# Gated attention and a two-way maxout layer on one core: fewer score groups of the first sequence computed on both sides of the diagonal, and two weight loads at other times

## The chip, the cores and the metric

The kernel runs on one core of a Trainium2 chip. A core has a matrix engine (TensorE, "PE" in the profile, its weight loads "PEld"), a vector engine (DVE), a scalar engine (ACT), a general engine (GpSimd, "POOL"), an engine that here only issues transfers (SyncE, "SP"), and 16 DMA engines that move data between the memory (HBM) and the on-chip buffer (SBUF), or within SBUF. TensorE writes its results to PSUM, which DVE and ACT read. The metric is the device time of one execution in microseconds (us); a run is repeated and the median is taken.

## The reference

There are eight sequences of 3072 tokens. `u` and `v` have 256 columns, `z` has 64; the layer behind has 1024 hidden columns.

```python
scores = (1 / S) * z @ z.T              # 3072 x 3072 for each of 8 sequences
attn   = maximum(scores, 0) ** 2
x      = u * (attn @ v)                 # 24576 tokens x 256
h1, h2 = x @ w1, x @ w2                 # 24576 x 1024 each
out    = maximum(h1, h2) @ w_out        # 24576 x 256
```

The matrix of scores is symmetric, because both factors are `z`. So is its squared positive part. A block of it that lies on one side of the diagonal, transposed, is the block at the mirrored place. The other identity that the kernel uses is `max(h1, h2) = max(h1 - h2, 0) + h2`: the difference needs only `w1 - w2`, and `h2 @ w_out` needs only the folded matrix `W2o = w2 @ w_out`.

## The kernel before, in words

**Tiles.** Tokens of a sequence are cut into 24 blocks of 128 (`NSB`), and these into six groups of four (`G = 4`, `NG = 6`). A step (`class Step`) is one group of 512 query tokens `s` of one sequence `b`; there are 48 steps. In a step, `xacc0` and `xacc1` in PSUM, one for each half of the 256 columns, add up 24 key blocks: each takes two matmuls 128x128 by 128x512, one for each half (`add`, `attn`). The operand that streams is a tile of squared positive scores; it comes from one of three places: `a_sb`, scored by this step itself (`add_own`); `aT`, scored by an earlier step of the same sequence and transposed by DMA (`add_early`); or `aD`, the diagonal group (`add_diag`).

**Scores.** `scores_pair(b, s, k0)` makes the scores of two key blocks against the 512 queries: two matmuls with 64 rows into one PSUM tile `s_ps`, a Relu on ACT (L218, into `r_sb`), a square on DVE (L221, into `a_sb`), and, if the key group lies behind the query group and is not scored again later, a transposing DMA on SP's queue into `aT` (L226). Pairs are made in windows of three (`WIN = 3`): the matmuls of three pairs back to back, which fill the three PSUM tiles of the pool `mm_psum`. In the first four steps the diagonal group is made by pairs as well (`NDIAG`).

**Who is scored twice.** `direct(b, i, j)` on L186 says which groups above the diagonal are not transposed, but scored again by the later step. In the first sequence these are all six pairs of groups among the first four (`i < j <= NDIR`, `NDIR = 3`): (0,1), (0,2), (0,3), (1,2), (1,3) and (2,3). In the other sequences there are none.

**The layer behind.** When a step has all 24 blocks, `finish` multiplies `xacc` by `uT`, the transposed `u`, on DVE (L268), which gives `xT`. Three steps later (`LAG = 3`) follow `put_d`, 16 matmuls `d_ps` with `w1 - w2`, with their Relu into `g_sb` (L292), and `put_o`, the product with `w_out` and `W2o` (`o_ps`, L323, and the store). `fold_w2o` makes `W2o` once, from `w_out` and from `w2T_sb`, which is `w2` transposed by DMA. The subtraction `w1 - w2` is one DVE instruction (L163).

**Order.** TensorE's order is written out: `work` is the list of its pieces with nominal costs, and `reads` says which score rows a piece needs and how long before it (`LAT_OWN`, `LAT_TURNED`, `LAT_DIAG`). From these, each window gets a place between the pieces, as late as its due time allows and at a distance from the others (`GAP`). In steps 1 to 3 of the first sequence the pieces next to a step's border go one column half after the other (`add_half`). `plan` and `plan_load` give transfers a place by nominal time after the start of a step: `plan_load(0, 0, 7, ...)` is 7 nominal us after step 0 of sequence 0 begins. A load is issued from POOL's queue, behind a one-column copy (`gate`, L83) that waits for the newest tile, so that the load does not start early. Transposes and stores are issued from SP's queue in program order, and one that must wait holds up those behind it. The matmuls, the SP transfers, the gates and the loads are all kept in program order (`pin`); the vector and scalar instructions mostly are not, and a scheduler places them.

Of the kernel before, what the change touches and what calls it, by code (L numbers as in the profile page):

```python
# [11 lines left out]
def kernel(  # L12
# [27 lines left out]
    P = 128  # L40
    NSB = S // P
    G = 4
    WIN = 3
    GW = G * P
    NG = NSB // G
    KD = D // P
    KF = Dff // P
    LAG = 3
    NDIR = 3
# [35 lines left out]
    def load(**kw):  # L85
        pin(nc.gpsimd.dma_start(**kw))
# [69 lines left out]
    w1_sb = consts.tile([P, KD, Dff], bf16)  # L156
    w2_sb = consts.tile([P, KD, Dff], bf16)
# [26 lines left out]


    def direct(b, i, j):  # L186
        return b == 0 and i < j <= NDIR


    def score(q, out_ps, j, k, s, q0, n):  # L190
# [13 lines left out]
    def scores_pair(b, s, k0):  # L204
        q = seqs[b]
        s_ps = mm_psum.tile([P, 2, GW], fp32, name="s_ps", tag="mm")
        for j in range(2):
            score(q, s_ps[:, j, :], j, k0 + j, s, 0, G)
        yield
        a_sb = apool.tile([P, 2, GW], bf16, name="a_sb")  # L210
        r_sb = apool.tile([P, 2, GW], bf16, name="r_sb", bufs=3)

        head = b == 0 and s == 0 and k0 < 10
        keep = pin if head else lambda ins: None
        if head and k0 in (2, 6):
            keep(nc.vector.tensor_single_scalar(out=r_sb, in_=s_ps, scalar=0.0, op=ALU.max))  # L216
        else:
            keep(nc.scalar.activation(r_sb, s_ps, AF.Relu))  # L218
        if head and k0 < 4:
            yield  # L220
        keep(nc.vector.tensor_mul(a_sb, r_sb, r_sb))  # L221
        gj = k0 // G
        if gj > s and not direct(b, s, gj):
            if (s, gj) not in q.T:
                q.T[s, gj] = tpool.tile([P, G, G, P], bf16, name="aT")
            turn(  # L226
                q.T[s, gj][:, ds(k0 - G * gj, 2), :, :].rearrange("p k q x -> p (k q) x"),
                a_sb.rearrange("p j q -> p (j q)"),
            )
        yield a_sb  # L230
# [123 lines left out]
    class Step:  # L354
        def __init__(self, b, s):
            self.b, self.s, self.q = b, s, seqs[b]
            self.xacc = None
            self.n = [0] * KD
            self.diag = not (b == 0 and s <= NDIAG)
            self.rows = ([None] if self.diag else []) + [  # L360
                k0
                for k0 in range(0, NSB, 2)
                if k0 // G > s or direct(b, k0 // G, s) or (k0 // G == s and not self.diag)
            ]
            self.early = [i for i in range(s) if not direct(b, i, s)]
            self.scored = {}
# [11 lines left out]
                self.n[dc] += 1  # L378
            attn(self.q, k, moving, self.xacc, dcs, n == 0, n == NSB - 1)

        def add_early(self, k):
            i, qb = divmod(k, G)
            self.add(k, self.q.T[i, self.s][:, :, qb, :])

        def add_own(self, k, dcs=range(KD)):
            self.add(k, self.scored[k - k % 2][:, k % 2, :], dcs)

        def add_half(self, ks, dc):
            for k in ks:
                self.add_own(k, [dc])  # L390

        def add_diag(self, j):
            self.add(G * self.s + j, self.scored[None][:, j, :, :])
# [26 lines left out]
    LAT_OWN, LAT_TURNED, LAT_DIAG = 2900, 9000, 10000  # L420

    def put(ns, shares, fn, reads=()):
        work.append((ns, shares, fn, reads))

    def put_early(st, ks):
        for k in ks:
            i = k // G
            rows = [((NG * st.b + i, k0), LAT_TURNED) for k0 in (G * st.s, G * st.s + 2)]
            put(432, False, lambda st=st, k=k: st.add_early(k), rows)

    def put_d(n):
        if n >= 0:
            for _ in range(KF // 2):
                put(864, True, steps[n].piece_d)

    def put_o(n, split=False):
        if n >= 0:
            for _ in range(G // 2):
                put(2180, True, lambda: steps[n].piece_o(split))

    for n, st in enumerate(steps):
        b, s = st.b, st.s
        if n:
            put(0, False, steps[n - 1].finish)
        put(0, False, st.begin if n else lambda: None, "begin")
        early = [G * i + j for i in st.early for j in range(G)]

        within = {}
        lat = LAT_OWN if n > LAG else 6 * 432
        if s == 0:  # L450
            put_o(n - LAG)
        elif s == NG - 1:
            put_d(n - LAG)
            put_early(st, early[: len(early) // 2])
            put_o(n - LAG)
            put_d(n - LAG + 1)
            put_early(st, early[len(early) // 2 :])
        elif early:
            put_d(n - LAG)
            put_early(st, early[:-2])  # L460
            put_o(n - LAG)
            put_early(st, early[-2:])
        elif n == LAG:
            within = {
                5: lambda: put_d(0),
                9: lambda: (put(1800, True, fold_w2o), put_o(0)),
            }
        own = [k0 for k0 in st.rows if k0 is not None]
        for i, k0 in enumerate(own):
            if i in within:  # L470
                within[i]()
            if not early and n <= LAG and i in ((0, 1) if n else ()) + (len(own) - 2, len(own) - 1):


                if i in (0, len(own) - 2):
                    ks = [own[i], own[i] + 1, own[i + 1], own[i + 1] + 1]
                    for dc in range(KD):
                        put(
                            864,
                            False,  # L480
                            lambda st=st, ks=ks, dc=dc: st.add_half(ks, dc),
                            [((n, own[i]), lat), ((n, own[i + 1]), lat)],
                        )
                continue
            for k in (k0, k0 + 1):
                put(432, False, lambda st=st, k=k: st.add_own(k), [((n, k0), lat)])
        if st.diag:
            for j in range(G):
                put(432, False, lambda st=st, j=j: st.add_diag(j), [((n, None), LAT_DIAG)])
# [50 lines left out]
    for w in reversed(range(len(windows))):  # L540
        limit = min([limit] + [due[r] for r in windows[w] if r in due])
        found = [i for i in spots if begins[i] <= limit]
        i = found[-1] if found else 0
# [11 lines left out]
    def plan(b, s, us, is_load, fn):  # L555
        transfers.append((start_of[b, s] + us * 1000, len(transfers), is_load, fn))

    def plan_load(b, s, us, fn):
        plan(b, s, us, True, fn)
# [14 lines left out]
    def fetch_v(b, i):  # L574
        load_v(b, seqs[b].v, i * G, G)

    for n, st in enumerate(steps):
        b, s = st.b, st.s
# [4 lines left out]
        if s == 0 and b + 1 < B:  # L583
            c = b + 1
# [7 lines left out]
            plan(b, *zT_at, False, lambda c=c: turn_z(c))  # L592
            for i, at in enumerate(v_at):
                plan_load(b, *at, lambda c=c, i=i: fetch_v(c, i))
    plan_load(0, 0, 7, lambda: load(out=w2_sb, in_=moe_w2.rearrange("(c p) f -> p c f", p=P)))
    plan_load(0, 1, 3, lambda: load(out=w1_sb, in_=moe_w1.rearrange("(c p) f -> p c f", p=P)))
    plan_load(0, 2, 9, lambda: load(out=w_out_sb, in_=moe_w_out.rearrange("(c p) d -> p c d", p=P)))
    plan(0, 2, 2, False, turn_w2)
    plan(0, 2, 6, False, subtract_weights)
# [84 lines left out]
```

## Time and profile before

| what | value |
|---|---|
| median of three runs | 981.61 us (981.32 to 990.35) |
| the profiled execution | 981.29 us |
| its span, from first to last instruction | 979.5 us |
| TensorE busy | 968.7 us, 99% |
| DVE busy | 432.2 us, 44% |
| ACT busy | 442.6 us, 45% |
| POOL busy | 77.7 us, 8% |
| granted TensorE clock | 1.00 |
| matmuls of scores of pairs, 128x512 into `s_ps` (with the diagonal's) | 696 |
| transposes into `aT` | 228 |

The span is what the profile can place; 1.8 us of the execution lie around it. An engine's busy time counts each moment once, however many of its instructions overlap. The timeline view merges like instructions that follow one another: start, length, engine, line, operation, output and inputs, count. The view of the transfers gives for each group of DMA issues the size and the time from issue to landing, that is until the data is in place and a waiting engine may go on.

In the first sequence the work of a step takes 13.8 us on TensorE as long as no piece of the layer behind is in it: step 1 begins at about 23.5 us, step 2 at 37.3 us, step 3 at 51.1 us.

### The profile page before, as it was taken

The numbers are of one execution on the slowest core, as the hardware profiler recorded it, in microseconds if no ns is written. First come the engines' busy times: TensorE is split into PE (matmuls) and PEld (weight loads), VectorE is DVE, ScalarE is ACT, GpSimd is POOL, SyncE is SP. The second block draws the span as 40 slices with busy tenths as digits, with TensorE's granted clock in tenths as the row PEclk, the third lists the DMA queues.
The fourth block names the chain that finished last, engine by engine and source line by source line (L and its number), as shares of the span: only waits on it lengthen the run. The fifth ranks groups of instructions, "written<-read, shape, count | busy, mean of one in ns | idle before, by whom it ended". The sixth has DMA issues, their size and how long they took to land.

```text
span 979.5 us, 14514 instructions
## 1 busy us (share of the span) xinstructions
PE 968.7 (99%) x5662; PEld 510.3 (52%) x5743; DVE 432.2 (44%) x681; ACT 442.6 (45%) x500; POOL 77.7 (8%) x228
## 2 busy tenths in 40 slices
PE   9999999999999999999999999999999999999998
PEld 3355545555455554555545564455545555445556
DVE  6654444443544435433445334444345443554322
ACT  6853454334643355433554335533355433654322
POOL 2011000110001100010000100011000110000000
PEclk9999999999999999999999999999999999999999
DMA  9999599987999969897788979889778796796621
GB/s 151 171 161 187 103 182 150 164 149 123 175 160 144 155 123 177 150 170 128 151 156 144 179 119 157 148 153 181 135 147 149 136 187 127 149 161 118 109 66 65
DMA packets 378517, 143.46 MB, mean 146 GB/s; under 512 B 356944, under 2 KB 358608, under 8 KB 378448
## 3 DMA queue, kind: packets, MB, share of 16 engines
q1 hardware_dynamic: 361888, 112.78, 61.5%
q0 software_dynamic: 16560, 29.74, 21.6%
q8 instruction: 45, 0.74, 0.3%
q14 instruction: 24, 0.20, 0.1%
HBM read 59.77 MB, written 25.17 MB: 87 GB/s over the span
## 4 chain that ended last, share of the span: by engine, by line
PE 99%; issue 1%; DVE 0%; ACT 0%
PE xacc L74 52%; PE o_ps L74 21%; PE d_ps L74 17%; PE s_ps L74 8%; PE w2o_ps L74 0%; ACT r_sb L218 0%; DVE r_sb L216 0%; PE tpz L134 0%; DVE a_sb L221 0%; DVE o_sb L317 0%; DVE blank L333 0%
## 5 line engine op out<-in xcount | busy, mean ns | idle before, releaser
L74 PEld LDWEIGHTS <-v_sb 128*128 128x128 bf16 x2304 | 215.9, 98 | 277.7 <-issue 41.1
L218 ACT ACTIVATE r_sb<-s_ps 128x1024 bf16<-128x1024 f32 x258 | 248.6, 1023 | 111.4 <-PE s_ps L74 111.2
L221 DVE TENSOR_TENSOR a_sb<-r_sb 128x1024 bf16<-128x1024 bf16 x260 | 179.4, 691 | 212.9 <-ACT r_sb L218 208.9
L74 PE MATMUL xacc<-a_sb,v_sb 128*128 128x512 bf16 x997 | 231.3, 379 | 2.5 <-issue 0.2
L74 PE MATMUL xacc<-aT,v_sb 128*128 128x512 bf16 x912 | 216.5, 379 | 0.0
L74 PE MATMUL o_ps<-w_out_sb,g_sb 128*128 128x256 bf16 x1536 | 199.1, 273 | 0.0
L74 PE MATMUL d_ps<-xT,w_sb 128*128 128x512 bf16 x751 | 172.7, 379 | 0.9
L74 PEld LDWEIGHTS <-g_sb 128*128 128x128 bf16 x1536 | 149.9, 98 | 27.6
L292 ACT ACTIVATE g_sb<-d_ps 128x1024 bf16<-128x1024 f32 x96 | 98.3, 1024 | 138.8 <-PE d_ps L74 138.8
L292 DVE TENSOR_SCALAR g_sb<-d_ps 128x1024 bf16<-128x1024 f32 x96 | 117.4, 1223 | 84.7 <-PE d_ps L74 81.3
L323 ACT COPY o_sb<-o_ps 128x512 f32<-128x512 f32 x94 | 55.1, 586 | 178.2 <-PE o_ps L74 178.2
L268 DVE SCALAR_TENSOR_TENSOR xT<-xacc,uT 128x512 bf16<-128x512 f32 x96 | 62.0, 683 | 137.4 <-PE xacc L74 137.4
L74 PEld LDWEIGHTS <-w_sb 128*128 128x128 bf16 x768 | 75.1, 98 | 88.7
L74 PE MATMUL s_ps<-zT 64*128 64x512 bf16 (+3 forms) x696 | 89.2, 359 | 0.1
L246 ACT ACTIVATE r_sb<-s_ps 128x896 bf16<-128x896 f32 x44 | 40.3, 917 | 97.9 <-PE s_ps L74 97.9
L74 PE MATMUL xacc<-aD,v_sb 128*128 128x512 bf16 x331 | 79.9, 379 | 2.6 <-issue 2.2
L74 PE MATMUL o_ps<-W2o_sb,xT 128*128 128x256 bf16 x384 | 73.3, 273 | 0.0
L248 DVE TENSOR_SCALAR r_sb<-s_ps 128x384 bf16<-128x384 f32 x44 | 24.6, 558 | 95.3 <-PE s_ps L74 95.3
L74 PEld LDWEIGHTS <-zT 64*128 64x128 bf16 x696 | 27.3, 94 | 62.6 <-issue 50.5
L83 POOL COPY gate_sb<-g_sb 128x1 bf16<-128x1 bf16 x44 | 8.3, 188 | 407.8 <-DVE g_sb L292 238.5
L74 PEld LDWEIGHTS <-xT 128*128 128x128 bf16 x384 | 37.6, 98 | 4.3
L83 POOL COPY gate_sb<-a_sb 128x1 bf16<-128x1 bf16 x48 | 9.7, 202 | 271.8 <-DVE a_sb L221 271.8
(37 smaller groups left out, 143.3 us busy)
## 6 DMA issues: line engine op xcount, KB each, us to landing
out_dram<-o_sb SPq DMA_DIRECT2D x47, 512.0 KB, 4.1
v_sb<-in_v_dram POOLq DMA_DIRECT2D x48, 256.0 KB, 5.9
u_sb<-in_u_dram POOLq DMA_DIRECT2D x48, 256.0 KB, 5.3
aT<-a_sb SPq DMA_TRANSPOSE x228, 3.6
z_sb<-in_z_dram POOLq DMA_DIRECT2D x7, 384.0 KB, 7.5
aD<-aD SPq DMA_TRANSPOSE x132, 2.4
w_sb<-in_moe_w_dram POOLq DMA_DIRECT2D x2, 512.0 KB, 7.5
uT<-u_sb SPq DMA_TRANSPOSE x48, 4.3
```

What stands on the lines that cost most here:

```text
L74: pin(nc.tensor.matmul(*args, **kw))
L83: pin(nc.gpsimd.tensor_copy(gate_sb, tile_ap))
L218: keep(nc.scalar.activation(r_sb, s_ps, AF.Relu))
L221: keep(nc.vector.tensor_mul(a_sb, r_sb, r_sb))
L246: nc.scalar.activation(r_sb, s_ps[:, 0:7, :], AF.Relu)
L248: nc.vector.tensor_single_scalar(out=r2_sb, in_=s2_ps[:, 2:5, :], scalar=0.0, op=ALU.max)
L268: nc.vector.scalar_tensor_tensor(out=xT[:, dc, :].rearrange("p (t q) -> p t q", q=P), in0=xacc[dc].rearrange("p (t q) -> p t q", q=P), sca ...
L292: nc.any.tensor_single_scalar(out=g_sb[:, nb : nb + 2, :], in_=d_ps, scalar=0.0, op=ALU.max)
L323: nc.any.tensor_copy(o_sb[:, ds(2 * th, 2), :], o_ps[:, :, :D])
```

## The change

Three things are edited.

1. `direct` now holds only for neighbours: (0,1), (1,2) and (2,3). The three groups farther from the diagonal, (0,2), (0,3) and (1,3), are scored once, by the earlier step, and transposed by DMA into `aT` for the later one. So steps 2 and 3 of the first sequence have "early" rows, as later steps have.
2. The order of pieces in those steps follows from that. Step 2 begins with the four blocks that it takes from `aT`, one column half after the other. Step 3 begins with `put_d(0)`, then six of its eight early blocks, then `fold_w2o` and `put_o(0)`, then the last two early blocks, and its own rows last. Before, step 3 began with own rows, and had `put_d(0)` after five pairs of own rows and `fold_w2o` and `put_o(0)` after nine.
3. The load of `w2` is planned 2 us after the start of step 1 and not 7 us after the start of step 0; the load of `w1` 9 us after the start of step 1 and not 3 us.

```diff
     def direct(b, i, j):
-        return b == 0 and i < j <= NDIR
+        return b == 0 and j == i + 1 and j <= NDIR
...
-        def add_early(self, k):
+        def add_early(self, k, dcs=range(KD)):
             i, qb = divmod(k, G)
-            self.add(k, self.q.T[i, self.s][:, :, qb, :])
+            self.add(k, self.q.T[i, self.s][:, :, qb, :], dcs)
...
         def add_half(self, ks, dc):
             for k in ks:
-                self.add_own(k, [dc])
+                (self.add_early if k // G in self.early else self.add_own)(k, [dc])
...
+    def reads_of(st, k, lat):
+        n, i = NG * st.b + st.s, k // G
+        if i in st.early:
+            return [((n - st.s + i, k0), LAT_TURNED) for k0 in (G * st.s, G * st.s + 2)]
+        return [((n, k - k % 2), lat)]
...
+    def put_border(st, ks, lat):
+        reads = sum((reads_of(st, k, lat) for k in ks), [])
+        for dc in range(KD):
+            put(864, False, lambda dc=dc: st.add_half(ks, dc), reads)
...
-        elif early:
+        elif n >= LAG:
             put_d(n - LAG)
             put_early(st, early[:-2])
+            if n == LAG:
+                put(1800, True, fold_w2o)
             put_o(n - LAG)
             put_early(st, early[-2:])
-        elif n == LAG:
-            within = {
-                5: lambda: put_d(0),
-                9: lambda: (put(1800, True, fold_w2o), put_o(0)),
-            }
...
+        else:
+            ks = (early + own)[:G] if n else []
+            if ks:
+                put_border(st, ks, lat)
+            early, own = early[G:], own[len(ks) if not early else 0 :]
+            put_early(st, early)
+        tail = own[-G:] if n + 1 < LAG else []
+        for k in own[: len(own) - len(tail)]:
+            put(432, False, lambda st=st, k=k: st.add_own(k), reads_of(st, k, lat))
+        if tail:
+            put_border(st, tail, lat)
...
-    plan_load(0, 0, 7, lambda: load(out=w2_sb, in_=moe_w2.rearrange("(c p) f -> p c f", p=P)))
-    plan_load(0, 1, 3, lambda: load(out=w1_sb, in_=moe_w1.rearrange("(c p) f -> p c f", p=P)))
+    plan_load(0, 1, 2, lambda: load(out=w2_sb, in_=moe_w2.rearrange("(c p) f -> p c f", p=P)))
+    plan_load(0, 1, 9, lambda: load(out=w1_sb, in_=moe_w1.rearrange("(c p) f -> p c f", p=P)))
```

The counts of instructions differ by this: 12 score matmuls of 64 rows and their 12 weight loads fewer on TensorE, six Relu fewer on ACT, six squares fewer on DVE, six transposes into `aT` more on SP. The 24 matmuls of those blocks into `xacc` read `aT` in place of `a_sb`. From step 4 on the order on every engine is the old one, but for a few gates, loads and one store that stand a few places away.

More of the change, by code (lines that the diff above doesn't have):

```diff
@@ L423, in put @@
         work.append((ns, shares, fn, reads))
+    def reads_of(st, k, lat):
[3 more added lines that the diff above has]
+        return [((n, k - k % 2), lat)]
     def put_early(st, ks):
         for k in ks:
-            i = k // G
-            rows = [((NG * st.b + i, k0), LAT_TURNED) for k0 in (G * st.s, G * st.s + 2)]
-            put(432, False, lambda st=st, k=k: st.add_early(k), rows)
+            put(432, False, lambda k=k: st.add_early(k), reads_of(st, k, 0))
+    def put_border(st, ks, lat):
+        reads = sum((reads_of(st, k, lat) for k in ks), [])
+        for dc in range(KD):
+            put(864, False, lambda dc=dc: st.add_half(ks, dc), reads)
     def put_d(n):
@@ L446 @@
         early = [G * i + j for i in st.early for j in range(G)]
-        within = {}
+        own = [k for k0 in st.rows if k0 is not None for k in (k0, k0 + 1)]
         lat = LAT_OWN if n > LAG else 6 * 432
@@ L457 @@
             put_early(st, early[len(early) // 2 :])
-        elif early:
+        elif n >= LAG:
             put_d(n - LAG)
             put_early(st, early[:-2])
+            if n == LAG:
+                put(1800, True, fold_w2o)
             put_o(n - LAG)
             put_early(st, early[-2:])
-        elif n == LAG:
-            within = {
-                5: lambda: put_d(0),
-                9: lambda: (put(1800, True, fold_w2o), put_o(0)),
-            }
[L468 to L486, printed above, removed]
+        else:
[9 more added lines that the diff above has]
+            put_border(st, tail, lat)
         if st.diag:
```

## The prediction

> **What bounds the kernel now.** I read the page first: the busy line, the chain, and the group of the score matmuls.
>
> ```profile
> PE 968.7 (99%) x5662; PEld 510.3 (52%) x5743; DVE 432.2 (44%) x681; ACT 442.6 (45%) x500; POOL 77.7 (8%) x228
> ...
> PE 99%; issue 1%; DVE 0%; ACT 0%
> ...
> L74 PE MATMUL s_ps<-zT 64*128 64x512 bf16 (+3 forms) x696 | 89.2, 359 | 0.1
> ```
>
> The chain that ended last is TensorE from start to end. So time falls by whatever TensorE work goes, unless TensorE then waits for something. The 696 score matmuls, 359 ns each, occupy 89.2 us: 0.128 us each, because the two of a pair, on 64 rows each, lie beside one another.
>
> Then the sums by stage, for steps 1 and 2 of the first sequence, as the change is all in the first 75 us:
>
> ```profile
> 23.50:37.30 13.80, 13.75 (x75) 5.22 (x72) 9.41 (x15) 11.42 (x13) 1.63 (x4) 1.00 1.04 163
> 37.30:51.10 13.80, 13.75 (x75) 5.21 (x72) 10.46 (x16) 11.42 (x13) 0.75 (x2) 1.00 1.24 183
> ```
>
> After the length stand the busy times of PE, PEld, DVE, ACT and POOL, the granted clock (1.00), the DMA share and GB/s. PE is full. ACT is at 11.42 of 13.80, but PE does not wait for it. DMA is the other resource without room: the packets' times sum to 1.04 and 1.24 of sixteen engines, which means that they overlap and hinder each other.
>
> **What goes.** The timeline of TensorE shows one period of a step:
>
> ```profile
> 33.33 0.82 PE L74 MATMUL s_ps<-zT 64*128 64x512 bf16 x6
> 34.09 2.76 PE L74 MATMUL xacc<-a_sb,v_sb 128*128 128x512 bf16 x12
> 36.78 0.82 PE L74 MATMUL s_ps<-zT 64*128 64x512 bf16 x6
> ```
>
> A window of three pairs holds PE from 33.33 to 34.09, 0.76 us; the 12 accumulating matmuls take 2.69. The change takes out six pairs, which are two windows: 2 x 0.76 = **-1.52 us**. (By the page's 0.128 us it is 12 x 0.128 = 1.54.) The matmuls into `xacc` stay, and read `aT` at the same price: 12 of them lie between 96.03 and 98.71 us, 2.68. Six Relu of 1023 ns and six squares of 691 ns go from engines that PE does not wait for: nothing.
>
> **What is added: six transposes on SP, and reads of them.** The nearest rows are in SP's own timeline and the transfers:
>
> ```profile
> 26.86 1.31 SPq L77 DMA_TRANSPOSE uT<-u_sb  x1
> 30.47 9.98 SPq L77 DMA_TRANSPOSE aT<-a_sb  x4
> 40.55 1.41 SPq L77 DMA_TRANSPOSE uT<-u_sb  x1
> 42.05 4.42 SPq L77 DMA_TRANSPOSE w2T_sb<-w_sb  x1
> ```
>
> Undisturbed, SP issues one in 1.29 us (median of the view of `aT` up to 75 us) and it lands 3.3 us later (its minimum). Beside loads, four take 9.98 us, 2.5 each, and land up to 8.7 us after issue. So six more cost SP 7.7 to 15 us before 50 us. Nothing on PE shows unless a reader comes first. The readers, by the changed order and the rows of before:
>
> - *Group (0,2)*. Read at the start of step 2, 37.5 us. Its rows are squared by 14 us, but SP first issues `uT` of step 0 at 15.03, as that waits for its load. Then the two go out by 16.4 + 2 x 2.5 = 21.4 and land by 30. Free.
> - *Groups (0,3), (1,3)*. Read from 53 us in step 3. At 2.5 us each all eight of step 0 are out by 36.4 and the two of (1,3) by 42.7, landed by 51.4. Free.
> - *Buffers of `a_sb`* (18). A square must wait for the transposes of the tile that lay there 18 tiles earlier: the 23rd square, at 32.3, for the first transpose, landed by 28; the 30th, at 40.2, for the last of step 0, landed at 36.4 + 4.4 = 40.8 at the slow rate and 32 at the fast. At most 0.6 us, on DVE; I take nothing.
> - *`uT` of step 2*. Queued behind everything above, and step 3's `xacc` waits for the product with it. Step 2 ends at 49.8 and `put_d(0)` covers 3.5 us, so the landing is needed by 51.9. At the fast rate it is issued at 35 (the last square of step 1 ends at 33.96), at the slow one, 16 issues after 15.03, at 54, and lands at 58; between, near 42, with landing at 47. From 0 to 6 us; I take 0, as `w2`'s load no longer lies beside step 0's transposes (two of those took 2.3 and 4.1 us to issue while it ran, the undisturbed 1.29).
> - *`w2T`*. It follows `uT`, takes 6.5 us to land, and is needed at 56.7. 0 to 6 us, the same queue; I take 0.
>
> **What moves.** `put_d(0)` stood at 56.52 us. Now it follows directly on the last 24 matmuls of step 2: 44.44 + 24 x 0.224 = 49.8, so 6.7 us earlier, while the loads it needs are later.
>
> - *`w1`*. The gate now stands on the third tile of the window at 33.33, squared at 37.62. POOL is free then, so the load goes out at 38.2 instead of 31.04. The subtraction keeps its place on DVE, behind the same nine squares:
>
> ```profile
> 47.07 0.69 DVE L221 TENSOR_TENSOR a_sb<-r_sb 128x1024 bf16<-128x1024 bf16 x1 [0.29 <-ACT r_sb L218]
> 47.68 1.22 DVE L163 TENSOR_TENSOR w_sb<-w_sb 128x2048 bf16<-128x2048 bf16 x1
> ```
>
> It starts at 47.7 and ends at 48.9; the first `d_ps` comes at 49.8. So `w1` must land by 48.5, 10.3 us after issue. The two loads of this size in the transfers before, at 20.69 and 31.04 us:
>
> ```profile
> w_sb<-in_moe_w_dram POOLq DMA_DIRECT2D x1, 512.0 KB, 6.2
> ...
> w_sb<-in_moe_w_dram POOLq DMA_DIRECT2D x1, 512.0 KB, 8.8
> ```
>
> It lands between 44.4 and 47.0, nearest the second, which also had transposes beside it (one took 8.2 us to land). No stall, with 1.5 us to spare. Behind the waiting subtraction DVE holds the two products of step 2, and PE waits for the subtraction itself. Cover gone, it costs the excess one for one: at 12 us to landing, 1.7.
> - *`w2`* goes out behind the load of `u` at 28 instead of 20.69 and lands by 37: early enough.
> - *`fold_w2o`* moves from 64.29 to 56.7 (49.8 + 3.46 of `d_ps` + 4 matmuls 0.9 + a window 0.76 + 8 matmuls 1.79). `w_out`'s gate takes the tile squared at 47.8, not 51.5, and the load goes out at 48.4. Its own row before is 7.9, which gives 56.3; with 8.8 it is 57.2. From nothing to 0.5 us of stall, more if the queue is worse; I take **+0.4**, as step 2's four transposes will lie beside it.
> - *The window after `put_d(0)`* comes after 4 matmuls and not 8. Its third pair needs the PSUM tile of the last `d_ps`; DVE's Relu of that (0.2 us after the matmuls, 1.23 long) ends at 54.7, when the pair is due. **+0.1**.
> - The store of step 0, the next loads of `z`, `v` and `u`: some us earlier, each with 10 us or more before its reader. Nothing. After step 4 all orders are as before.
>
> Sum against the profiled execution: 981.29 - 1.52 + 0.4 + 0.1 = 980.27. The median, 981.61, stands 0.32 above the profiled one, so I say **980.6**.
>
> **The Trainium skill** has two rules here that the numbers above do not use. "DMA: Bandwidth & Descriptors", section "Anatomy of one DMA", fits a load from POOL as about 2.0 us plus its bytes over 436 GB/s. An estimate by it, for the 1 MB that `w1` is in HBM, is 4.4 us; the trace has 6.2 and 8.8, so the measurement decides, and by the page no load would ever be late and the sum would be 979.9. The same page, section "Issuing engines are not separate DMA queues", speaks against the change: SP's transposes and POOL's loads share the same 16 DMA engines. The trace agrees (8.8 for the load beside three transposes).
>
> **Rivals.**
>
> *B. The transposes jam the DMA engines, and TensorE waits at about 50 us.* Place: `put_d(0)` for `w1`, or the first `xacc` of step 3 for `uT`. For it: the DMA share of 1.24, and 2.5 us per transpose. Against it: `w2` and `w1` are now apart, and no PE wait for a DMA shows today. It decides from 1.5 us of stall; the slow rate throughout gives 58 + 0.7 of the product against 53.3, 5.4 us, so 981.6 - 1.5 + 5.4 = 985.5, slower than before; half of that gives 982.8. "TensorE: Matmul & The Clock Gate", Part 1, says that an idle window of about 3.4 us halves the clock; no run here shows it (clock 1.00 in every row), and it would add about 2 us to the longest stall.
>
> *C. Nothing gained: what PE saves turns into small waits* (`w_out`, PSUM, DVE), since these are each within 1 us of due. 981.3 to 981.9. For it: ACT at 83% of a step, and window after window close to due. Against: today these waits sum to 2.5 us of `xacc` in the whole run.
>
> *D. The gain whole*: no wait at all. 981.61 - 1.52 = 980.1; with each window's switch saved as well (16 `d_ps` matmuls take 3.46 us, 0.216 each; the period of 3.45 less 12 of those is 0.86) 979.9.
>
> **How the numbers follow.** Forecast (a stall of 0.2 to 1.2) 0.40, D 0.22, C 0.13, B 0.22, and 0.03 for a jam over 10 us. The range drops the upper end of B and the 0.03: low 979.3 (D, less 0.5 for the spread of medians), high 984.0. About 1% is what a measurement of this kernel can tell from no change; all cases but the last are within it: faster 0.01 and slower 0.01 for what no case holds, slower 0.03 for the jam, same 0.95.
>
> **What would show it.** Right: PE busy about 1.5 us less, 684 score matmuls and 234 transposes; `d_ps` first at about 49.8 us, `fold_w2o` at 56.7; the subtraction at 47.7 with no DMA named before it. Wrong: an idle PE between 49 and 58 us, with DVE's L163 or L268 named as releaser and a load or `uT` behind that; a `w1` load that takes over 10 us; or transposes that SP issues at over 2 us each up to 50 us.

## The result, and the profile after

The changed kernel is slower: 992.17 us in the median of ten runs (987.61 to 996.7, and one far outlier of 1692, at a granted clock of 0.56 over the whole execution), against 981.7 for the kernel before. The ratio is 1.0095, with a 95% interval from 1.0066 to 1.0124. The forecast was 980.6 with a range from 979.3 to 984.0, so time and sign were wrong. The profiled execution took 995.36 us, its span is 993.6, which is 14.1 us more than before. It is the second longest of the nine without the outlier, so its waits are probably longer than those of a typical execution.

The page of the changed kernel: the busy line, the chain, and the groups of the accumulation that reads `aT` and of the product with `uT`.

```profile
PE 973.0 (98%) x5650; PEld 511.3 (51%) x5731; DVE 427.6 (43%) x675; ACT 436.8 (44%) x494; POOL 78.3 (8%) x228
...
PE 93%; DMA 3%; issue 1%; SPq 1%; DVE 1%; ACT 1%; POOL 0%; DVEq 0%; POOLq 0%; ACTq 0%
...
L74 PE MATMUL xacc<-aT,v_sb 128*128 128x512 bf16 x936 | 223.5, 380 | 5.7 <-DVE xT L268 5.7
...
L268 DVE SCALAR_TENSOR_TENSOR xT<-xacc,uT 128x512 bf16<-128x512 f32 x96 | 61.8, 683 | 147.6 <-PE xacc L74 127.7
```

Two things show at once. The chain was 99% TensorE, and is 93% with 3% of DMA in it. And TensorE is busy 4.3 us *longer*, with 12 matmuls fewer, worth 1.5 us: so its work was stretched by 5.8 us. The rest of the 14.1 us, 9.8, is idle time. These three numbers are the whole account: -1.5 + 5.8 + 9.8 = 14.1.

Where the idle time lies is told by the waits of the first 130 us (who waited for whom: sum, times, longest):

```profile
DVE xT L268 <- DMA uT<-u_sb: 11.9, 3, 6.7
...
PE xacc L74 <- DVE xT L268: 5.7, 4, 3.1
PE xacc L74 <- DMA aD<-aD: 3.7, 1, 3.7
```

and by TensorE's timeline at these places:

```profile
37.48 0.82 PE L74 MATMUL s_ps<-zT 64*128 64x512 bf16 x6
40.46 1.02 PE L74 MATMUL xacc<-aT,v_sb 128*128 128x512 bf16 x4 [2.16 <-DVE xT L268]
41.66 1.02 PE L74 MATMUL xacc<-aT,v_sb 128*128 128x512 bf16 x4 [0.17 <-DVE xT L268]
...
52.87 3.62 PE L74 MATMUL d_ps<-xT,w_sb 128*128 128x512 bf16 x15
59.58 0.38 PE L74 MATMUL xacc<-aT,v_sb 128*128 128x512 bf16 x1 [3.09 <-DVE xT L268]
60.18 1.26 PE L74 MATMUL xacc<-aT,v_sb 128*128 128x512 bf16 x3 [0.22 <-DVE xT L268]
...
102.36 2.72 PE L74 MATMUL xacc<-aD,v_sb 128*128 128x512 bf16 x6 [3.72 <-DMA aD<-aD]
104.88 5.25 PE L74 MATMUL d_ps<-xT,w_sb 128*128 128x512 bf16 x16
```

Steps 2 and 3 cannot start to accumulate, because DVE waits for the transposed `u` of the step before; step 4 cannot end, because its diagonal tiles have not come back from the transpose. The sums by stage after the second and third of these stalls show the other loss, in the third number from the end, the granted clock:

```profile
59.60:65.40 5.80, 5.41 (x18) 1.46 (x17) 4.66 (x6) 2.85 (x3) 0.00 (x0) 0.71 1.29 156
...
102.40:110.00 7.60, 7.60 (x23) 2.79 (x23) 2.51 (x3) 1.72 (x2) 0.00 (x0) 0.62 0.75 178
```

A clock of 0.71 over 5.8 us and of 0.62 over 7.6 us is 1.7 + 2.9 us of lost clock; before, it was 1.00 in every row. In the last rows 16 `d_ps` matmuls took 5.25 us, not 3.62. Some of the rest lies at the start: the first `xacc` of step 0 came at 8.87 us and not 8.18. That differs from execution to execution: over the thirteen profiles here it lies between 8.07 and 9.30 us.

Why `uT` is late stands in SP's own timeline:

```profile
16.63 13.06 SPq L77 DMA_TRANSPOSE aT<-a_sb  x8
29.78 3.34 SPq L77 DMA_TRANSPOSE uT<-u_sb  x1
33.21 15.20 SPq L77 DMA_TRANSPOSE aT<-a_sb  x6
48.51 4.75 SPq L77 DMA_TRANSPOSE uT<-u_sb  x1
53.35 5.50 SPq L77 DMA_TRANSPOSE w2T_sb<-w_sb  x1
```

Step 0's eight transposes went out in 13.06 us, 1.6 each. Step 1's six took 15.20, 2.5 each, and `uT` of step 2 left at 48.51 and landed 9.8 us later, at 58.3. In the view of the transfers, at 42 to 44 us, issue to landing was this:

```profile
w_sb<-in_moe_w_dram POOLq DMA_DIRECT2D x1, 512.0 KB, 8.0
aT<-a_sb SPq DMA_TRANSPOSE x1, 12.1
...
u_sb<-in_u_dram POOLq DMA_DIRECT2D x1, 256.0 KB, 11.1
aT<-a_sb SPq DMA_TRANSPOSE x1, 12.4
```

The load of `w1` and that of `u` for step 3, 2.5 us behind it, lay beside the last transposes of step 1. Each of those took 12 us where an undisturbed one takes 3.2.

### The profile page after: what moved, and what is told of

It reads as the page before. It is cut to its first block, busy times and chain, and to the rows that moved or that the text cites. A ratio compares the mean times of both kernels' runs of the same rounds, so it can differ in the third digit from the quotient of the medians.

```text
span 993.6 us, 14489 instructions
## 1 busy us (share of the span) xinstructions
PE 973.0 (98%) x5650; PEld 511.3 (51%) x5731; DVE 427.6 (43%) x675; ACT 436.8 (44%) x494; POOL 78.3 (8%) x228
## 4 chain that ended last, share of the span: by engine, by line
PE 93%; DMA 3%; issue 1%; SPq 1%; DVE 1%; ACT 1%; POOL 0%; DVEq 0%; POOLq 0%; ACTq 0%
PE xacc L74 49%; PE o_ps L74 21%; PE d_ps L74 16%; PE s_ps L74 7%; DMA w2T_sb<-w_sb 1%; DMA uT<-u_sb 1%; DMA aD<-aD 1%; SPq L77 1%; ACT r_sb L218 1%; DVE a_sb L221 0%; DMA o_sb<-in_z_dram 0%; PE w2o_ps L74 0%; DVE r_sb L216 0%; PE tpz L134 0%; DVE xT L268 0%
## 5 line engine op out<-in xcount | busy, mean ns | idle before, releaser
L218 ACT ACTIVATE r_sb<-s_ps 128x1024 bf16<-128x1024 f32 x252 | 243.0, 1023 | 118.2 <-PE s_ps L74 116.7
L221 DVE TENSOR_TENSOR a_sb<-r_sb 128x1024 bf16<-128x1024 bf16 x254 | 175.0, 691 | 220.5 <-ACT r_sb L218 216.4
L74 PE MATMUL xacc<-aT,v_sb 128*128 128x512 bf16 x936 | 223.5, 380 | 5.7 <-DVE xT L268 5.7
L74 PE MATMUL xacc<-a_sb,v_sb 128*128 128x512 bf16 x975 | 225.3, 379 | 2.4 <-issue 0.2
```

The source lines that it names most:

```text
L74: pin(nc.tensor.matmul(*args, **kw))
```

## The experiments

**First question: the transposes or the loads?** Two theories. Theory 1: six more transposes are too much for the queue wherever the loads are. Theory 2: the loads of `w1` and `w2`, which the change moved in beside the transposes, make the jam. Four kernels take the parts apart.

*The changed kernel, loads at the old places* (`e1_old_load_times`):

```diff
-    plan_load(0, 1, 2, lambda: load(out=w2_sb, ...
-    plan_load(0, 1, 9, lambda: load(out=w1_sb, ...
+    plan_load(0, 0, 7, lambda: load(out=w2_sb, ...
+    plan_load(0, 1, 3, lambda: load(out=w1_sb, ...
```

> The changed kernel with the loads of w1 and w2 back at their old places. Theory 1 (six more transposes are too much for SP's queue wherever the loads lie): the uT products of steps 1 and 2 still come late, 986 to 994 us. Theory 2 (the load of w2, moved beside the transposes of uT of step 1, and that of w1, moved beside step 2's, make the jam): uT of step 1 lands before 38 us, no PE idle time before step 3, 980 to 983 us.

Measured: 985.93 us, ratio 1.0045 (1.0023 to 1.0067). Better than the changed kernel, but slower than before. The profile has one stall of TensorE for a late `uT`, 3.95 us at step 2, with the clock at 0.63 for the 4.6 us that follow, and 0.9 us for `w_out`. `uT` of step 1 left SP at 33.8, behind eight transposes that the load of `w2` had slowed, and landed at 41.5; it is needed at 38. Neither theory's range holds the median. The late `uT` of step 1 is theory 1's wait; that of step 2, which theory 1 had late as well, came in time.

*The kernel before, with only the loads moved* (`e2_loads_only`): the reverse edit on the old kernel.

> The kernel before with the loads of w1 and w2 at their new places and nothing else changed. Theory 1: with four transposes per step the queue has room; 981 to 982.5 us. Theory 2: uT of step 1 or 2 lands late as in the changed kernel and PE waits at the start of steps 2 or 3; 984 to 992 us.

Measured: 999.14 us, ratio 1.0158 (1.0118 to 1.0198). The half of the change that I had priced at nothing costs more alone than the whole change. No transpose is added here, and yet:

```profile
44.08 7.84 SPq L77 DMA_TRANSPOSE w2T_sb<-w_sb  x1
52.01 8.06 SPq L77 DMA_TRANSPOSE aT<-a_sb  x4
60.16 4.35 SPq L77 DMA_TRANSPOSE uT<-u_sb  x1
64.60 23.55 SPq L77 DMA_TRANSPOSE aT<-a_sb  x4
```

This is SP's timeline. Four transposes take 23.55 us to issue, 5.9 each. The backlog that began behind `w1` meets the loads of `w_out`, `u`, `z` and `v` one after the other, and never drains: from 75 to 85 us the DMA share is 1.38 and only 90 GB/s move, against 234 in the kernel before in these ten microseconds (first this run, then the kernel before; the DMA share and GB/s stand last):

```profile
75.00:85.00 10.00, 9.92 (x53) 4.10 (x51) 6.52 (x12) 4.57 (x5) 1.44 (x4) 1.00 1.38 90
75.00:85.00 10.00, 10.00 (x59) 4.71 (x58) 7.11 (x14) 4.77 (x6) 1.62 (x5) 1.00 1.19 234
```

In this stretch the engines were busier and moved less. TensorE pays at 89 us (3.9 us for `aT`) and at 106 us (6.9 us for `aD`), long after the loads that began it.

*The changed kernel without its six transposes* (`e3_no_far_transposes`): the far groups come from a tile of zeros.

```diff
-        if gj > s and not direct(b, s, gj):
+        if b == 0 and s + 1 < gj <= NDIR:
+            q.T[s, gj] = far_sb
+        elif gj > s and not direct(b, s, gj):
```

> The changed kernel without its six transposes: the three far groups are read from a tile of zeros, so their part of the sum is left out; the matmuls and the load times are those of the changed kernel. Theory 1: no late uT, the 1.5 us of the two windows is gained whole, 980 to 981 us. Theory 2: uT of step 1 still waits behind the load of w2, 984 to 990 us.

Measured: 985.72 us, ratio 1.0037 (1.0018 to 1.0057), single runs from 981.4 to 990.1. Theory 2's range, but by another wait: `uT` of step 2 landed at 53.0 and stalled TensorE by 0.2 us only. The loss came 40 us later: 2.75 us for `aD` at 94.7, and a clock of 0.54 in the 3.5 us behind it. So the new load places alone keep the gain from coming.

*The kernel before plus the six transposes* (`e4_before_plus_six`), into tiles that nobody reads:

```diff
-        if gj > s and not direct(b, s, gj):
+        if gj > s and (gj > s + 1 or not direct(b, s, gj)):
```

> The kernel before with the six transposes added, into tiles that nobody reads; scores, order and load times are the old ones. Theory 1: uT of steps 1 or 2 lands late, 984 to 992 us. Theory 2: the queue carries them, at most 1 us, 981.5 to 982.5 us.

Measured: 986.4 us; ratio 1.0024, with an interval (0.9966 to 1.0082) that does not tell it from no change. Its profile has one stall, at the start of step 2, for `uT` of step 1:

```profile
37.09 0.82 PE L74 MATMUL s_ps<-zT 64*128 64x512 bf16 x6
40.80 1.02 PE L74 MATMUL xacc<-a_sb,v_sb 128*128 128x512 bf16 x4 [2.88 <-DVE xT L268]
```

All five executions, 985.0 to 990.1, lie above the median of the kernel before, 982.2. Both theories were half right. The transposes with the old loads cost a wait of 3 to 4 us at one place. The new load places cost much more than that in the old order of pieces (`e2_loads_only`) and as much in the new one (985.72 in `e3_no_far_transposes`, 985.93 in `e1_old_load_times`), at places that wander.

**Second question: is anything else in the change slow, and is it the loads in flight or the transposes by themselves?**

*The order alone* (`e5_order_alone`): no far transposes, loads at the old places.

> The changed kernel without its six transposes (the three far groups are read from a tile of zeros, so their part of the sum is left out) and with the loads of w1 and w2 at the old places. What is left of the change is the two windows less and the new order of pieces. Theory (both the transposes and the new load places fill the DMA queues, and nothing else costs): no late uT, 979.8 to 981.0 us, 1.2 to 1.9 below before. Rival (the new order itself waits, for w_out, PSUM or DVE): 981.5 us or more.

Measured: 980.79 us against 982.08 for the kernel before on the same chip, 1.3 below; ratio 0.9992 (0.9983 to 1.0001). The interval just holds no change. The profile has no wait of TensorE for a transfer but 0.3 us for `w_out`. Its span is that of the kernel before, 979.5 us, but its first `xacc` came at 9.30 us and not 8.18; from there on it is 1.1 us shorter, near the 1.5 of the sum less that wait. So the new order itself costs nothing that shows.

With this run there are four medians for the changed order: 980.79 with neither the six transposes nor the new load places, 985.93 with the transposes alone, 985.72 with the load places alone, and 992.17 with both. Each costs about 5 us alone, and a little over 6 beside the other.

*Six transposes, but `w1` and `w2` never loaded* (`e8_no_weight_loads`): constants are written on chip in their place.

> The changed kernel with its six transposes, but w1 and w2 are set to constants on chip and never loaded, so the layer behind computes with other weights. Theory (a load in flight beside the transposes makes these slow): SP issues them at 1.3 us each, uT of steps 1 and 2 land in time, 980 to 983 us. Rival (six more transposes are too much by themselves): late uT as before, 986 us or more.

Measured: 981.04 us, and 979.79 in the profiled execution, whose span is 978.0: 1.5 below the 979.5 of before, the whole gain. The ratio is 1.001 (0.9983 to 1.0037), as three of ten executions take 988 to 992. SP's timeline in this run, to be laid beside that of the changed kernel:

```profile
16.69 12.91 SPq L77 DMA_TRANSPOSE aT<-a_sb  x8
29.70 3.19 SPq L77 DMA_TRANSPOSE uT<-u_sb  x1
32.98 8.16 SPq L77 DMA_TRANSPOSE aT<-a_sb  x6
41.24 2.59 SPq L77 DMA_TRANSPOSE uT<-u_sb  x1
```

The same six transposes of step 1 need 8.16 us and not 15.20, and `uT` of step 2 leaves 7.3 us earlier. So the six transposes are not too much by themselves in this execution; it is the loads of `w1` and `w2` in flight beside them that make them slow. What delays the three long executions is not shown, as none of them was profiled.

**Third question: is it one transfer at the wrong place in the queue, or the sum of transfers?** Here `uT` for steps 1 to 3 is issued some five transposes earlier.

```diff
-        plan(b, s, 1, False, lambda b=b, s=s: turn_u(b, s))
+        early_u = b == 0 and 0 < s <= 3
+        plan(b, s - early_u, 3 if early_u else 1, False, lambda b=b, s=s: turn_u(b, s))
```

*With the old load places* (`e6_ut_early_old_loads`):

> The changed kernel with the loads at the old places, and the transposes of u for steps 1 to 3 of the first sequence issued from SP some five transposes earlier. Theory (late uT at the end of SP's queue is what the readers wait for, not a lack of DMA in sum): the stall of 3.9 us at step 2 and the halved clock behind it go, 980.5 to 982 us. Rival (the sum of DMA work is too much): the wait moves to aT, w2T, w_out or aD, 984 us or more.

*With the new ones* (`e7_ut_early`):

> The changed kernel with its own load places and the transposes of u for steps 1 to 3 issued some five transposes earlier. Theory (late uT): the stalls of 2.3 and 3.3 us at steps 2 and 3 go, 983 to 987 us, with a wait left for aD at about 100 us. Rival (sum of DMA work): as the changed kernel, 988 us or more.

Measured: 986.31 us, ratio 1.0044 (1.0025 to 1.0064), and 990.14, ratio 1.0111 (1.0069 to 1.0152). TensorE waited for `uT` no more in either profile, but for `w2T`, 9.1 and 7.6 us. The timeline of the first:

```profile
55.12 1.90 PE L74 MATMUL xacc<-aT,v_sb 128*128 128x512 bf16 x8
66.09 3.59 PE L74 MATMUL w2o_ps<-w_out_sb,w2T_sb 128*128 128x256 bf16 x16 [9.07 <-DMA w2T_sb<-w_sb]
```

`w2T` had kept its place in SP's queue, behind 14 transposes into `aT` as in the changed kernel. In the first run it was issued at 51.9 us, between the loads of `w_out` (49.1) and `u` (54.4), and took 14.2 us to land; in `e1_old_load_times` it went out at 50.3, before `w_out`, and took 4.4. It landed at 66.0 and 64.3 us, near the 65.4 of the changed kernel, where the earlier stalls had hidden it. The rival held: the other order of this queue chose who was late.

*Two loads apart* (`e9_u3_later`): the kernel before with the new places of `w1` and `w2`, but the load of `u` that went out 3.3 us behind `w1` is planned 5 us later.

> The kernel before with the loads of w1 and w2 at the new places (the run that took 991 to 1001 us), and the load of u for step 3, which there went out 3.3 us behind w1's, moved 5 nominal us later. Theory (the transposes starve while loads follow one another without a break; uT of step 2 was caught behind w1 and u): uT of step 2 lands by 50 us, no pile-up behind it, 982 to 986 us. Rival (the place of w1's load alone does it): 990 us or more.

Measured: 984.76 us; ratio 1.0009 (0.9971 to 1.0047), where it had been 1.0158. Its executions scatter from 981.3 to 997.1. `uT` of step 2 landed at 50.7 in place of 52.3, later than the 50 expected, and the pile-up behind it mostly stayed away (a wait of 2.0 us for `aD`). A single 256 KB load, moved by some 7 us, is worth 14 us. The transposes that were issued beside `w1` alone, at 38.5 and 39.9 us, still took 11.3 and 10.8 us to land, so one load is enough to slow them; what the gap behind `w1` saved lay in the backlog after it. That it is the unbroken row of loads that hurts, more than any one of them, fits this; no run had `w1` at its old place and `w2` at the new one, or the reverse.

**Can the change be saved?** `e10_spread` has the old load places, `uT` early, `w2T` right behind `uT` of step 2, and the loads of `z` and `v` for the second sequence later:

```diff
-    plan(0, 2, 2, False, turn_w2)
+    plan(0, 1, 3.1, False, turn_w2)
...
-                z_at, zT_at = (3, 5), (4, 4)
-                v_at = [(3, 9), (3, 14), (4, 0), (4, 5), (4, 9), (4, 13)]
+                z_at, zT_at = (3, 10), (4, 3)
+                v_at = [(4, 2), (4, 6), (4, 10), (4, 14), (5, 2), (5, 6)]
```

> The changed kernel with w1 and w2 loaded at the old places, uT of steps 1 to 3 issued some five transposes earlier, w2T issued right behind uT of step 2, and the loads of z and v for the second sequence 5 to 15 nominal us later. Theory (each wait seen so far was one transfer caught behind loads that could be moved): no wait of PE for DMA, 980.2 to 981.5 us. Rival (the sum of transfers before 75 us is too much, the wait only moves): 983 us or more.

Measured: 981.31 us against 982.09, ratio 0.9993 (0.9967 to 1.0019); eight of twelve executions are below 982.2, four between 983 and 987. The profiled one was one of the latter, with waits for `w_out` (2.6) and `aD` (1.3), where the theory had none. `e11_spread_more` moves these as well, and puts `uT` of step 3 back to its old place:

```diff
-            plan_load(b, s, 2 if b == 0 else 4, lambda nx=nx: fetch_u(nx.b, nx.s))
+            plan_load(b, s, (9 if s == 2 else 2) if b == 0 else 4, lambda nx=nx: fetch_u(nx.b, nx.s))
...
-    plan_load(0, 2, 9, lambda: load(out=w_out_sb, ...
+    plan_load(0, 1, 12, lambda: load(out=w_out_sb, ...
...
-                v_at = [(4, 2), (4, 6), (4, 10), (4, 14), (5, 2), (5, 6)]
+                v_at = [(4, 10), (4, 15), (5, 0), (5, 4), (5, 8), (5, 12)]
```

> The run with the transfers spread, and further: w_out is loaded into the pause behind w1, before the u of step 3, which goes out 7 nominal us later; the loads of v for the second sequence begin 8 nominal us later still. Theory (each remaining wait is one transfer caught behind loads): the waits of 2.6 us for w_out and 1.3 us for aD go, nearly all executions at 980 to 981 us. Rival (the sum of transfers is too much): executions of 983 us and more stay as frequent as 4 in 12.

Measured: 981.16 us against 981.73, ratio 0.9998 (0.9976 to 1.002). The profiled execution took 980.01, with a span of 978.2 and no wait of TensorE for a transfer; eight of twelve are at 980 to 981.3, but four are still at 983 to 988, as many as the rival had. So a gain of up to 1.5 us is there in most executions, and the others give it back; what delays these is not shown. No version beats the kernel before beyond its interval.

## Why the prediction was wrong, point by point

- **What goes, -1.52 us: right.** The span is 978.0 in `e8_no_weight_loads`, 1.5 below that of before, and the median of `e5_order_alone` is 1.3 lower, with an interval that just holds no change.
- **"`uT` of step 2 ... I take 0": the term that failed.** I had put its landing between 39 and 58 us, and chose 47. It landed at 58.3, the far end, and cost 3.3 us. That it met the number 58 is luck: it left at 48.5 and not at 54, and took 9.8 us to land and not 4.4. The reason given for the choice was that `w2` no longer lay beside step 0's transposes. That was true (1.6 us each there), and beside the point: the load had moved beside step 1's, and beside `uT` of step 1. Of the two rows given for it, only that of 4.1 us was issued during `w2`'s load; that of 2.3 was issued at 16.87, before the load at 20.69.
- **`uT` of step 1 was not on the list of readers**, and was the first to be late. It has the same place in the queue one step earlier. It left at 29.78, right behind the loads of `u` (28.27) and `w2` (29.29), landed at 39.6, and cost 2.3 us. A list of readers has to hold every transfer behind the added ones, not the added ones and the last.
- **"`w2` ... lands by 37: early enough"** looked at the load's own reader and priced nothing for its neighbours. It landed at 38.7, early enough indeed. The price of the two moved loads to the others is about 5 us in the changed order without the six transposes, 6 with them, and 17 in the old order (`e2_loads_only`). This is the largest miss. The rule that I cited from the Trainium skill ("DMA: Bandwidth & Descriptors", "Issuing engines are not separate DMA queues") says that these share the engines. I had set it beside a load that transposes slowed; for what the moved loads do to the transposes, the sum had no term.
- **"`w2T` ... I take 0": wrong, and hidden.** It took 12.1 us to land and not 6.5, at 65.4 us. TensorE waited only 0.2 us for it, as it was late already; in `e6_ut_early_old_loads` the like cost 9.1.
- **The store, `z`, `v` and later `u`: "each with 10 us or more before its reader. Nothing. After step 4 all orders are as before."** The order was, the queues were not empty. Three of these loads went out at 66.2, 67.0 and 67.7 us, as all three gates waited for the tile that DVE squared at 64.9; a transpose issued between them took 13.4 us to land; `aD` was 3.7 us late at 102 us.
- **`w1`: right.** Issued at 41.6 and not 38.2, as the stall of 2.3 us and the later start came first, it took 8.0 us, and the subtraction did not wait for it in the changed kernel. `put_d(0)` came at 52.87 = 49.8 + 0.7 (later start) + 2.3 (stall of step 2). `w_out` cost nothing, as the earlier stalls gave it time.
- **Rival B named the mechanism and one of the places**, with a chance of 0.22 and a price of up to 5.4 us, which reached 985.5. What it lacked: the other two places, and a rate. Its slow rate, 2.5 us for an issue and 8.7 to landing, was the worst row of before taken as the bound. Under two loads in a row it was exceeded: 12 to 13 us to landing here, up to 20 us and 5.9 us per issue in `e2_loads_only`. A bound read from a profile in which the resource just sufficed is no bound for one in which it does not.
- **The clock** I left out of the sum, as no row showed it. The changed kernel lost 4.6 us by it. "TensorE: Matmul & The Clock Gate", Part 1, has it half after an idle window of about 3.4 us. In the runs the length of the wait alone does not decide: the clock fell behind waits of 3.1, 3.7 and 3.95 us, but also behind 2.75 (`e3_no_far_transposes`) and 2.6 (`e10_spread`), and stayed at 1.00 behind 2.16 and 2.9 (`e4_before_plus_six`). What the traces show is a grid: every stretch at half clock behind these waits is 3.41, 6.83 or 10.24 us long, one, two or three times 3.41, and the stretches between them are whole multiples of it too. Each fall follows an interval of this grid in which TensorE was idle for 2.4 us or more. The grid cuts the 2.9 us of `e4_before_plus_six` into 1.2 and 1.7, and the clock stayed; the most idle interval that it survived in these stages had 1.8. For the second stall of the changed kernel, these are the interval before the fall, with TensorE busy for 0.60 us, and the one after it, at a clock of 0.50:

```profile
56.99:60.40 3.41, 0.60 (x3) 0.20 (x3) 1.57 (x3) 0.00 (x0) 0.56 (x2) 1.00 1.38 194
60.40:63.81 3.41, 3.38 (x12) 0.79 (x10) 2.67 (x3) 1.79 (x2) 0.00 (x0) 0.50 1.31 142
```

Open remains why a transpose beside loads is so much slower than its share would make it. The trace has packets of 256 bytes for the transposes, and of 2048 bytes for the loads of `u`, `v`, `w1` and `w2`. In the middle of the kernel before, from 300 to 700 us, they take 25 and 239 ns in the mean; in `e2_loads_only` between 78 and 88 us, 93 and 279. The Trainium skill ("DMA: Bandwidth & Descriptors", "Queues, rings and completion order") says that a DMA engine serves its queues in turn, a packet at a time; then, if the trace's packets are the page's, a small packet would wait for a large one at each turn. That the small ones are slowed nearly fourfold and the large ones hardly fits this, but no run here changed the size of packets, so it is argued and not shown.

## What to carry to other kernels

When a transfer is moved, price what it does to the transfers that it comes to lie beside, and not only whether it reaches its own reader in time; follow the queue behind it to the first time that it is empty. Here SP's first pause behind the load of `w1` at 41.6 us came at 108.1, some 65 us later. Where the DMA share of a stage is above 1 (1.24 here), the durations read in it are no upper bounds for one in which transfers are added. For a gain of 1.5 us, with transfers that stand within a few microseconds of their readers, look at the scatter of single executions as well as at their median.

## What was not expected of the hardware

- Loads and transposes in a backlog moved less at a higher DMA share: 90 GB/s at 1.38 (`e2_loads_only`, 75 to 85 us), 234 GB/s at 1.19 in the kernel before over the same stretch.
- The jam does not come out the same twice. Of the kernel before, 81 of 94 executions lie between 981.2 and 982.9 us, the others between 983.9 and 997.5; the variants with a late transfer in their profile scatter over 5 us or more (the changed one from 987.6 to 996.7), with the same program.
- Waits of 3 to 4 us cost TensorE two thirds as much again in clock as in idle time: 4.6 us of clock behind 6.8 us of waits in the changed kernel.
